# A fused attention and two-layer expert kernel: a least length for TensorE's runs of network products, and the plan's lengths of attention steps set anew

## The chip, the cores and the metric

One core of one Trainium2 chip runs the whole kernel. The metric is device time in microseconds (us), the median of the runs of one program. The engines are TensorE (PE in the profile; PEld is its weight load), VectorE (DVE), ScalarE (ACT), GpSimd (POOL) and SyncE (SP), which issues most DMA transfers.

## The reference

Attention on q, k and v of shape (4, 8, 576, 64), the sum of a pooled part and a banded part, feeds two networks one after the other; everything is float32.

```python
# pooled: mean over 4 neighbours, full attention on 144 positions, repeated 4 times
out_up = np.repeat(sm_attn(q_d, k_d, v_d), 4, axis=2)
# banded: softmax over the positions with |i - j| < 4
mask = np.abs(pos[:, None] - pos[None, :]) < 4
scores = np.where(mask, scale * np.matmul(q, k.transpose(0, 1, 3, 2)), -1e9)
x = (out_up + softmax(scores) @ v)            # as 2304 tokens x 512
g = x @ w_gate                                 # 512 -> 1536
x = (g * sigmoid(g) * (x @ w_val)) @ w_out     # 1536 -> 512
h = np.maximum(x @ w_in, 0.0)                  # 512 -> 2048
return h * h @ w_out2                          # 2048 -> 512
```

## The kernel before

The 2304 tokens are cut into nine tiles of 256 (`T1`). A float32 product is made of three float32r matmuls of 128x256 (`three`, lines 1045 to 1047), on operands split into a high and a low half. A product step of the first network (`gate`, `val` or `out_` in `unit_tasks`) is twelve of them: four blocks of 128 rows, three matmuls each. It is the unit in which network products are ordered. The first two tiles have four units (three product steps each) at first, later tiles six.

Attention makes the tiles. For each of the four batches there are four pooled tasks (`global_tasks`: one score step for two pairs of heads, then for each of its two halves a transpose step and a value step, lines 797, 816 and 835) and six banded tasks (`local_task`: a score step at line 649, a transpose step at line 686, a value step at line 707; the masked form of the first two batches also has one or two bfloat16 matmuls at line 644). Between these steps DVE and ACT do the softmax. The score and value steps work on 64 or 72 rows, the banded transposes on all 128, the pooled transposes on 72. `to_x` (line 725) adds both parts into the tile `xt`, of which there are two; when a tile is whole, ACT and DVE split it into `xs` (lines 1015 and 1019) and its product steps can begin.

The order of all instructions is worked out by a planner when the program is built (class `Order`). It keeps a clock for each engine, a list of times at which buffers come free, and for each task a list of `Stage`s with an engine, a planned length, and the buffers that it takes and gives. `next` takes the engine whose earliest stage starts first, lets all stages that could start within `LOOK` of it compete (0.05 us on TensorE), and decides by `rank`. On TensorE attention goes ahead of products as long as the attention steps since the last product (`streak`) are planned at less than `ATT_MAX`, 2.0 us; then products go first. `run` emits the chosen stage, so what it picks is the order in which each engine's queue is filled, SP's and POOL's DMA queues among them. Before a planned clock of 40 us `fill`, and up to 100 us `fill_bank`, put matmuls on zeros (lines 1251 and 81) where TensorE would wait. Nothing at run time reorders: a wrong planned length shows as a wait, or as a result that lies ready.

Four PSUM banks serve attention (`N_ATT`), two hold `gate` and `val` (`N_GV`), five buffers `p` and two `pt` pass the softmax on. Behind attention (270 us on) the rest of the span is network products alone.

Of the kernel before, what the change touches and what calls it, by code (L numbers as in the profile page):

```python
# [22 lines left out]
POOL = 4  # L23
# [27 lines left out]
QB = 1  # L51
# [12 lines left out]
def attn_moe_kernel(ctx: ExitStack, tc: tile.TileContext, qT, kT, vw, vin, vp, qp, kp, qs, ks, vs, maskc, masks, identc, wB, wC, out):  # L64
# [34 lines left out]
        return size / RATE  # L99

    AFTER = {"v": 0.15, "a": 0.2, "p": 0.2, "t": 0.25}
    ATT_MAX, LOOK_V, LOOK_A, LOOK_P, LOOK_T, LOOK_D, PE_MARGIN = 2.0, 0.1, 0.0, 0.2, 0.05, 0.6, 0.1
    PAD_END, PAD_WAIT, PAD_SHARE = 100.0, 0.6, 0.8
    TICK, FILL_END, BUSY = 10.24 / 3, 40.0, 3180
    W_DUE0, W_STEP, X_DUE0, X_STEP, X_STEP0 = 17.0, 2.2, 12.0, 20.0, 14.0
    S_DUE, S_STEP = 140.0, 15.0
    CUT_T, CUT_J, W_LAG, Q_LATE, Q_LATER, MASK_PE = 2, 4, 65.0, 10.0, 6.0, 2
    V_LATE, V_LATE1, V_LATE0, V_LEAD, W_LEAD, LEAD, LATE = -15.0, -10.0, -5.0, 1000.0, 1000.0, 80.0, 500.0
# [18 lines left out]
    def after(ts):  # L127

        return max([0.0] + [t.ready for t in ts]) if all(t.done for t in ts) else None

    class Order:
        def __init__(self):
            self.flying = []
            self.queues = {k: [] for k in ("x", "qk", "sum", "rows", "v", "att", "w", "mlp", "other", "done", "put")}
            n = {"att": N_ATT, "y": N_Y, "gv": N_GV, "p": N_P, "pt": N_PT, "v": N_V, "xt": N_XT}
            n |= {"sg": N_SG}
            self.free = {k: [0.0] * c for k, c in n.items()}
            self.named = {k: [(0.0, i) for i in range(n_[0])] for k, n_ in NAMED.items()}
            self.got = {k: [] for k in NAMED}
            self.clock = {e: 0.6 for e in "vaptd"}  # L140
            self.pad = 0
            self.load, self.filler, self.streak, self.landed = {}, None, 0.0, 0.0

        def hot(self, t):
# [59 lines left out]
        def next(self):  # L204

            found = {}
            heads = [(q[0], q) for q in self.queues.values() if q]
            for task, q in [(t, None) for t in self.flying] + heads:
                t = self.start(task)
                if t is None:  # L210
                    continue
                e = task.stages[task.at].engine
                if e is None:
                    return task, q, t, None
                wait = PE_MARGIN if e == "t" and not task.products else 0.0
                found.setdefault(e, []).append((max(t + wait, self.clock[e]), task, q, t))
            assert found, "no stage can go on"
            first = min(found, key=lambda e: min(c[0] for c in found[e]))
            limit = min(c[0] for c in found[first]) + LOOK[first]

            def rank(c):
                task = c[1]
                if task.products:
                    return (1 if first == "t" and self.streak < ATT_MAX else -1), task.due
                return 0, task.due

            _, task, q, t = min((c for c in found[first] if c[0] <= limit), key=rank)
            return task, q, t, first

        def run(self):  # L230
            while self.flying or any(self.queues.values()):
                task, q, t, engine = self.next()
                if q is not None:
                    q.pop(0)
                    self.flying.append(task)
                if task.at == 0:
                    self.flying += task.then
                s = task.stages[task.at]
                if engine == "t" and (task.products or self.clock["t"] >= FILL_END) and self.clock["t"] < PAD_END:
                    self.fill_bank(t, s)  # L240
                for k in s.take:
                    if k in self.named:
                        slot = min(self.named[k])
                        self.named[k].remove(slot)
                        self.got[k].append(slot[1])
                    else:
                        self.free[k].remove(min(self.free[k]))
                if engine == "t" and self.clock["t"] < FILL_END:
                    self.fill(max(t, self.clock["t"]), task)
                s.fn()  # L250
                if engine is not None:
                    c, cost = max(t, self.clock[engine]), s.cost
                    if engine == "t":
                        cost = self.columns(c, cost, s.share)
                        self.streak = 0.0 if task.products else self.streak + cost
                    self.clock[engine] = c + cost
                    t = c + cost + AFTER.get(engine, 0.0) + s.late
                    if engine == "d":

                        t = self.landed = max(c + FLIGHT, self.landed) + cost  # L260
                        self.clock["d"] = max(c + ISSUE, self.landed - AHEAD)
                        t += SLACK if c > FIRST else 0.3
                    if engine == "p":

                        self.landed = max(c + FLIGHT, self.landed) + dma(128 * HP * SD) * ACC
                        self.clock["d"] = max(self.clock["d"], self.landed - AHEAD)
                        t = max(t, self.landed + SLACK)
                task.ready = t
                task.times.append(t)
                task.at += 1  # L270
                for k in s.give:
                    if callable(k):
                        name, slot = k()
                        self.named[name].append((t, slot))
                    else:
                        self.free[k].append(t)
                if task.done:
                    self.flying.remove(task)
# [67 lines left out]
    att = tc.alloc_tile_pool(name="att", bufs=1)  # L346
# [267 lines left out]
    def local_task(b, i, ins, due, bls=(0, 1), early=False):  # L614

        u = {}
        first, last = early and i == 0, early and i == 2
# [8 lines left out]
        nb, b0 = len(bls), bls[0]  # L626
        n = nb * HP
# [118 lines left out]
        v_take = () if last else ("v",)  # L746
        v_in = Task([Stage("d", dma(128 * 512) * (1 if b < NB else 2), values, v_take, cond=lambda: task.ready)], due)
        if mask_pe:
            cost, share = 0.737 * nb, 0.74
            softmax = softmax_stages(u, n, 128, WIN, "s", float(D) ** -0.5, 1, False, ("att",))  # L750
        else:
            cost, share = 0.63 * nb, 0.68
            softmax = [Stage("v", dve(n * WIN), masked, (), ("att",))]
            softmax += softmax_stages(u, n, 128, WIN, "p", 1.0, 1, False, ())
        p_take, pt_take, pt_give = ("p",), ("pt",), ("pt",)
        if early:
# [6 lines left out]
                Stage("t", 0.22 * nb, trans, ("att",) + pt_take, p_take[-1:] * (not early), turn, 0.98),  # L763
                Stage("a", act(n * WIN, True), turned, (), ("att",)),
                Stage(
                    "t", 0.64 * nb, pv, ("att",), pt_give + v_take, ready, 0.62
                ),
                Stage("v", dve(232 * nb), to_x, (), ("att",)),
            ],
# [7 lines left out]
    def global_tasks(b, ins, due, combos, end=False):  # L777

        us = {}
        n = len(combos)  # L780
        cost = n * 0.26 * (POOL if b < QB else 1)

        def scores():
            for h2 in range(2):
                us[h2]["ps"] = bank("att")
                us[h2]["s"] = us[h2]["ps"][:QC, : n * SD].rearrange("p (c k) -> p c k", k=SD)
            for ci, (hp, qc) in enumerate(combos):
                for i in range(POOL if b < QB else 1):
                    for h2 in range(2):
                        r = slice(64 * h2, 64 * h2 + 64)  # L790
                        if b < QB:
                            c = qc * S // 2 - HALF0[qc] + i
                            q = q_t[b, qc][r, hp, c : c + S // 2 - POOL + 1 : POOL]
                        else:
                            q = qd_t[b][r, hp, qc * QC : qc * QC + QC]
                        start, stop = i == 0, b >= QB or i == POOL - 1
                        nc.tensor.matmul(us[h2]["s"][:, ci], q, kd_t[b][r, hp, :], start=start, stop=stop)  # L797

        first = Task(
            [Stage("t", cost, scores, ("att", "att", "p", "p"), (lambda: ("ys", 0),) * end, lambda: after(ins + [consts]), 0.92)],  # L800
            due,
        )
        for h2 in range(2):
            us[h2] = {}
            first.then = (*first.then, global_task(b, h2, us[h2], [first], due, combos))
        return first

    def global_task(b, h2, u, ins, due, combos):
        n = len(combos)
# [33 lines left out]
        def to_g():  # L843
            for r in range(2):
# [12 lines left out]
        task = Task(  # L857
            softmax_stages(u, n, QC, SD, "s", scale, POOL, True, ("att",), lambda: after(ins))
            + [
                Stage("t", 0.12 * n, trans, ("att", "pt"), ("p",), share=0.54),  # L860
                Stage("a", act(w, True), turned, (), ("att",)),
                Stage("t", (0.15 if apart else 0.2) * n, pv, ("att",), ("pt",), lambda: after(v_need), 0.84),
                Stage("a", halves * 0.051 + n * QC / 1200, to_g, (), ("att",)),
            ],
            due,
# [1577 lines left out]
```

## Time and profile before

| | |
|---|---|
| median of 3 runs | 943.97 us (943.89 to 944.54) |
| the profiled execution | 943.21 us, of which the span of the profile is 941.4 us |
| PE busy | 931.3 us, 99% |
| DVE busy | 758.2 us, 81% |
| ACT busy | 583.4 us, 62% |
| mean granted TensorE clock | 0.999 |

A busy PE says little here, since matmuls are pipelined and a matmul of 128x256 is shown with 0.28 us while one starts every 0.118 us. What matters is the distance from one matmul's start to the next one's, read from the order in time.

### The profile page before, as it was taken

What the parts mean: (1) busy time and instruction counts of PE and PEld (TensorE: products, weight loads), DVE (VectorE), ACT (ScalarE), POOL (GpSimd) and SP (SyncE); (2) the same over time, 40 slices, a digit from 0 to 9 for tenths busy, and PEclk for the clock granted to TensorE, in tenths of its full rate; (3) what the DMA queues carried; (4) which work ended last, traced back from release to release, by engine and by line L of the source; (5) the groups of instructions that cost most, each with busy time, mean ns of one, the idle gap of its engine ahead of it and who ended that gap; (6) DMA issues with size and microseconds to landing.
All of it is one profiled execution on the core that took longest, in us unless ns stands there. A gap on an engine that the chain in (4) does not pass through costs nothing.

```text
span 941.4 us, 22569 instructions
## 1 busy us (share of the span) xinstructions
PE 931.3 (99%) x8929; PEld 906.5 (96%) x8929; DVE 758.2 (81%) x1875; ACT 583.4 (62%) x1368; POOL 23.8 (3%) x31
## 2 busy tenths in 40 slices
PE   8999999999999999999999999999999999999997
PEld 7888999999999999999999999999999999999997
DVE  7998979778977788888896999968777667786775
ACT  4878566757666888466543575757565645445553
POOL 0102102000000000000000000000000000000000
PEclk9999999999999999999999999999999999999999
DMA  9998969485788756167462638614414864516131
GB/s 303 258 292 217 255 166 261 158 295 155 254 284 279 245 177 238 65 224 223 169 210 75 235 132 316 236 74 171 146 57 179 315 228 175 180 67 247 46 134 68
DMA packets 101205, 183.82 MB, mean 195 GB/s; under 512 B 22380, under 2 KB 60012, under 8 KB 101100
## 3 DMA queue, kind: packets, MB, share of 16 engines
q1 hardware_dynamic: 97644, 174.42, 54.7%
q0 software_dynamic: 3456, 7.96, 4.8%
q8 instruction: 70, 1.15, 0.5%
q14 instruction: 35, 0.29, 0.1%
HBM read 120.75 MB, written 61.60 MB: 194 GB/s over the span
## 4 chain that ended last, share of the span: by engine, by line
PE 96%; DVE 2%; ACT 1%; issue 0%; DVEq 0%
PE gv L1045 11%; PE gv L1046 11%; PE gv L1047 11%; PE y L1045 8%; PE y L1046 8%; PE y L1047 8%; PE att L1982 6%; PE att L1981 6%; PE att L1980 6%; PE att L1046 3%; PE att L1047 3%; PE att L1045 3%; PE att L707 2%; PE att L649 2%; PE att L797 2%; PE y L1251 2%
## 5 line engine op out<-in xcount | busy, mean ns | idle before, releaser
L1045 PE MATMUL gv<-xs,wg 128*128 128x256 f32 x880 | 250.5, 285 | 0.1
L1046 PE MATMUL gv<-xs,wg 128*128 128x256 f32 x880 | 247.0, 281 | 0.0
L1047 PE MATMUL gv<-xs,wg 128*128 128x256 f32 x880 | 246.8, 280 | 0.0
L1045 PEld LDWEIGHTS gv<-xs,wg 128*128 128x128 f32 x880 | 166.2, 189 | 2.3 <-DVE sg L1089 0.4
L1047 PEld LDWEIGHTS gv<-xs,wg 128*128 128x128 f32 x880 | 166.0, 189 | 0.0
L1046 PEld LDWEIGHTS gv<-xs,wg 128*128 128x128 f32 x880 | 166.0, 189 | 0.0
L2131 ACT ACTIVATE f<-rr 128x512 fp32r<-128x512 f32 (+2 forms) x200 | 87.8, 467 | 68.2 <-PE att L1982 32.2
L1982 PE MATMUL att<-wg,f 128*128 128x256 f32 x432 | 122.5, 284 | 0.5 <-DVE f L2134 0.4
L1980 PE MATMUL att<-wg,f 128*128 128x256 f32 x432 | 121.7, 282 | 0.3 <-ACT f L2131 0.3
L1981 PE MATMUL att<-wg,f 128*128 128x256 f32 x432 | 122.0, 282 | 0.0
L2134 DVE TENSOR_TENSOR f<-rr,f 128x512 fp32r<-128x512 f32 (+2 forms) x200 | 94.6, 490 | 29.5 <-ACT f L2131 28.4
L2055 ACT ACTIVATE rr<-rr 128x512 f32<-128x512 f32 (+1 forms) x144 | 79.8, 556 | 36.8 <-DVE rr L2058 35.0
L1046 PE MATMUL y<-xs,wg 128*128 128x256 f32 x336 | 94.7, 282 | 1.1 <-DVE xs L1570 1.1
L1045 PE MATMUL y<-xs,wg 128*128 128x256 f32 x336 | 94.6, 281 | 0.0
L1047 PE MATMUL y<-xs,wg 128*128 128x256 f32 x336 | 94.3, 281 | 0.0
L1982 PEld LDWEIGHTS att<-wg,f 128*128 128x128 f32 x432 | 81.2, 188 | 1.4 <-DVE f L2134 1.3
L1980 PEld LDWEIGHTS att<-wg,f 128*128 128x128 f32 x432 | 81.8, 189 | 0.6 <-ACT f L2131 0.6
L1981 PEld LDWEIGHTS att<-wg,f 128*128 128x128 f32 x432 | 81.5, 189 | 0.0
L2140 DVE TENSOR_TENSOR rr<-rr 128x256 f32<-128x256 f32 (+1 forms) x160 | 62.6, 393 | 9.1 <-ACT rr L2055 7.1
L1046 PEld LDWEIGHTS y<-xs,wg 128*128 128x128 f32 x336 | 63.5, 189 | 1.5 <-DVE xs L1570 1.5
L1045 PEld LDWEIGHTS y<-xs,wg 128*128 128x128 f32 x336 | 63.6, 189 | 0.4 <-ACT ys L1228 0.2
L1047 PEld LDWEIGHTS y<-xs,wg 128*128 128x128 f32 x336 | 63.5, 189 | 0.0
(149 smaller groups left out, 2316.8 us busy)
## 6 DMA issues: line engine op xcount, KB each, us to landing
wst<-wB SPq DMA_DIRECT2D x36, 512.0 KB, 5.0
w_sp<-tmp SPq DMA_DIRECT2D x36, 512.0 KB, 3.6
wg<-w_sp SPq DMA_DIRECT2D x36, 512.0 KB, 4.9
wst<-wC SPq DMA_DIRECT2D x32, 512.0 KB, 5.2
y_sp<-ys SPq DMA_DIRECT2D x29, 512.0 KB, 4.5
xf_sp<-xs SPq DMA_DIRECT2D x24, 512.0 KB, 2.7
xs<-xf_sp SPq DMA_DIRECT2D x24, 512.0 KB, 5.8
ys<-y_sp SPq DMA_DIRECT2D x20, 512.0 KB, 6.8
```

The lines of the kernel that those rows point to most:

```text
L649: nc.tensor.matmul(u["s"][r, c * HP + hp], q[r, hp, q0 - o : q0 - o + WIN], k[r, hp, w0 - o : w0 - o + WIN], start=not mask_pe, stop=not m ...
L707: nc.tensor.matmul(ps[rr, o : o + t1 - t0], u["v"][rr, bls[c], hpp, h2, :], pt[rr, c, hpp, h2, t0 - q0 : t1 - q0], start=True, stop=True,)
L1045: nc.tensor.matmul(o, w[:, 0], x[:, 0], start=start, stop=False, skip_group_check=more)
L1046: nc.tensor.matmul(o, w[:, 0], x[:, 1], start=False, stop=False, skip_group_check=more)
L1047: nc.tensor.matmul(o, w[:, 1], x[:, 0], start=False, stop=stop, skip_group_check=more)
L1980: nc.tensor.matmul(o, h, w[:, 0], start=first and not again and c == 0, stop=False, skip_group_check=again)
L1981: nc.tensor.matmul(o, h, w[:, 1], start=False, stop=False, skip_group_check=again)
L1982: nc.tensor.matmul(o, l, w[:, 0], start=False, stop=end, skip_group_check=again)
L2055: return lambda: nc.scalar.activation(out=whole(f, c0), in_=whole(f, c0), func=func)
L2131: nc.scalar.activation(out=fac(k, 0), in_=source(), func=AF.Copy)
L2134: nc.vector.tensor_tensor(out=fac(k, 1), in0=source(), in1=fac(k, 0).bitcast(F32), op=ALU.subtract)
L2140: go = lambda: nc.vector.tensor_tensor(out=o(), in0=a(), in1=b(), op=op)
```

## The change

The diff changes the planner and nothing of what is computed. `ATT_MAX` goes from 2.0 to 4.0 us. The planned clock gets 0.1 us (`SWITCH`) whenever TensorE goes from products to attention or back. A new count, `stay`, holds the planned length of products since the last attention step; from a planned clock of 70 us on, and while no attention step has run since the last product, products go ahead of attention until it has reached 4.0 us. The planned lengths of the attention steps are new: for two blocks of a banded task the masked scores go from 1.474 to 1.30 us, the others from 1.26 to 1.08, values from 1.28 to 1.07; for one block they go from 0.737 to 0.83, 0.63 to 0.61 and 0.64 to 0.60; the pooled scores go from 2.08 to 2.34 us in the first batch and from 0.52 to 0.64 in the others, a pooled transpose step from 0.24 to 0.25 and a pooled value step from 0.3 to 0.4.

```diff
-    ATT_MAX, LOOK_V, LOOK_A, LOOK_P, LOOK_T, LOOK_D, PE_MARGIN = 2.0, 0.1, 0.0, 0.2, 0.05, 0.6, 0.1
+    ATT_MAX, LOOK_V, LOOK_A, LOOK_P, LOOK_T, LOOK_D, PE_MARGIN = 4.0, 0.1, 0.0, 0.2, 0.05, 0.6, 0.1
+    SWITCH, STAY, STAY_FROM = 0.1, 4.0, 70.0
-            self.pad = 0
+            self.pad, self.stay, self.mode = 0, 0.0, False
                 if task.products:
-                    return (1 if first == "t" and self.streak < ATT_MAX else -1), task.due
+                    stay = self.stay < STAY and self.clock["t"] > STAY_FROM and self.streak == 0.0
+                    return (1 if first == "t" and self.streak < ATT_MAX and not stay else -1), task.due
                     if engine == "t":
+                        c += SWITCH * (self.mode != task.products)
+                        self.mode = task.products
                         cost = self.columns(c, cost, s.share)
+                        self.stay = self.stay + cost if task.products else 0.0
                         self.streak = 0.0 if task.products else self.streak + cost
-            cost, share = 0.737 * nb, 0.74
+            cost, share = 0.36 + 0.47 * nb, 0.74
-            cost, share = 0.63 * nb, 0.68
+            cost, share = 0.14 + 0.47 * nb, 0.8
-                    "t", 0.64 * nb, pv, ("att",), pt_give + v_take, ready, 0.62
+                    "t", 0.13 + 0.47 * nb, pv, ("att",), pt_give + v_take, ready, 0.74
-        cost = n * 0.26 * (POOL if b < QB else 1)
+        cost = n * (1.17 if b < QB else 0.32)
-                Stage("t", 0.12 * n, trans, ("att", "pt"), ("p",), share=0.54),
+                Stage("t", 0.125 * n, trans, ("att", "pt"), ("p",), share=0.54),
-                Stage("t", (0.15 if apart else 0.2) * n, pv, ("att",), ("pt",), lambda: after(v_need), 0.84),
+                Stage("t", (0.2 if apart else 0.25) * n, pv, ("att",), ("pt",), lambda: after(v_need), 0.84),
```

## Rows read from the trace of the kernel before

**Rows 1.** The page: span, and busy time of each engine.
```profile
span 941.4 us, 22569 instructions
...
PE 931.3 (99%) x8929; PEld 906.5 (96%) x8929; DVE 758.2 (81%) x1875; ACT 583.4 (62%) x1368; POOL 23.8 (3%) x31
```
**Rows 2.** Stretches: length, busy PE, PEld, DVE, ACT, POOL, clock, DMA share, GB/s.
```profile
33.90:68.77 34.87, 34.85 (x455) 31.09 (x455) 32.80 (x88) 26.08 (x75) 4.29 (x5) 1.00 0.97 292
68.77:107.67 38.90, 38.67 (x532) 34.86 (x529) 36.38 (x95) 30.79 (x86) 7.82 (x9) 1.00 0.94 240
107.67:158.97 51.30, 51.28 (x682) 48.05 (x680) 41.91 (x118) 34.35 (x100) 6.94 (x8) 1.00 0.82 209
```
**Rows 3.** PE in time order (start, us, line, tiles, shape, count): one product run between visits.
```profile
152.51 0.28 PE L1047 MATMUL y<-hh,wg 128*128 128x256 f32 x1
152.63 0.60 PE L686 MATMUL att<-ident,p 128*128 128x128 f32 x4
152.98 0.36 PE L1045 MATMUL gv<-xs,wg 128*128 128x256 f32 x1
153.18 0.28 PE L1046 MATMUL gv<-xs,wg 128*128 128x256 f32 x1
...
154.36 0.28 PE L1047 MATMUL gv<-xs,wg 128*128 128x256 f32 x1
154.56 1.14 PE L707 MATMUL att<-pt,vw 64*64 64x58 f32 x32
155.64 0.66 PE L686 MATMUL att<-ident,p 128*128 128x128 f32 x4
156.22 1.15 PE L649 MATMUL att<-kT,qT 64*64 64x64 f32 x32
157.30 0.39 PE L1045 MATMUL y<-hh,wg 128*128 128x256 f32 x1
```
**Rows 4.** PE in time order: one value step alone, then like steps side by side.
```profile
131.23 0.47 PE L835 MATMUL att<-pt,vd 72*64 72x72 f32 x8
131.63 0.44 PE L816 MATMUL att<-ident,p 72*72 72x72 f32 x4
...
140.26 0.72 PE L835 MATMUL att<-pt,vd 72*64 72x72 f32 x16
140.91 2.08 PE L649 MATMUL att<-kT,qT 64*64 64x64 f32 x64
142.92 0.39 PE L1045 MATMUL y<-hh,wg 128*128 128x256 f32 x1
```
**Rows 5.** PE in time order: first and last of 48 attention visits from 70 us.
```profile
71.80 0.72 PE L835 MATMUL att<-pt,vd 72*64 72x72 f32 x16
...
268.69 1.14 PE L707 MATMUL att<-pt,vw 64*64 64x58 f32 x32
```
**Rows 6.** Time order, all engines: the last steps before the third tile's products.
```profile
99.61 1.15 PE L649 MATMUL att<-kT,qT 64*64 64x64 f32 x32
...
106.83 0.68 DVE L1019 TENSOR_TENSOR xs<-xt,xs 128x512 fp32r<-128x512 f32 x1
```
**Rows 7.** PE in time order: where a long product run halts.
```profile
161.78 0.28 PE L1047 MATMUL gv<-xs,wg 128*128 128x256 f32 x1
162.13 0.39 PE L1045 MATMUL gv<-xs,wg 128*128 128x256 f32 x1
162.35 0.28 PE L1046 MATMUL gv<-xs,wg 128*128 128x256 f32 x1
```
**Rows 8.** Groups of PE instructions (count, busy us, mean ns, idle before): zeros that fill waits.
```profile
L81 PE MATMUL gv<-zeros 128*128 128x256 bf16 x21 | 2.6, 273 | 0.0
```
**Rows 9.** Waits (who, for whom: us, times, longest): first 70 to 300 us, then all.
```profile
PE att L835 <- ACT pt L822: 0.2, 1, 0.2
...
PE y L1046 <- DVE xs L1570: 1.1, 2, 0.6
PE y L1045 <- ACT ys L1228: 0.8, 1, 0.8
```

## The prediction

> **What bounds the kernel now.** First the page: TensorE is busy 931.3 of 941.4 us, the next engine, DVE, 758.2 [rows 1]. So the end is set by what TensorE's queue holds and how closely it runs, and a shorter attention step elsewhere is worth nothing by itself. Second the waits: from 70 to 300 us TensorE waited 0.2 us for anybody; over the whole span the longest sums are 1.1 and 0.8 us, both after attention [rows 9]. So almost nothing is to be had from waits where the change acts. Third the stretches: while attention runs, the clock is 1.00 and TensorE full, but DVE is at 32.80 of 34.87 and 36.38 of 38.90 us in the first two of them and 41.91 of 51.30 in the third [rows 2]. It is a second engine near its limit early on. Fourth the order in time, which shows what a full TensorE hides. Inside a run of products one matmul starts every 0.118 us (153.18 to 154.36 is ten). The first one of a run holds the second up until 0.20 us after it, and the last one is followed by a 64-row step 0.20 us after its start, but by a 128-row transpose 0.12 us after it (152.51 to 152.63) [rows 3]. So each visit of attention costs 0.08 us on the way back to products, and 0.08 us on the way in if it begins with a 64-row step. The run of twelve in the rows takes 1.58 us from start to start, 0.16 more than 12 x 0.118. That is what the change can win.
>
> **The visits removed.** From 70 us there are 48 visits [rows 5] and between them 47 product runs with 1,092 matmuls: 35 runs of 12 matmuls, four of 24, eight of 36 to 144 (576 matmuls in all). The new rule lets attention in only after 4.0 us of products. A product step is planned at 12 x 0.118 = 1.41 us, two are 2.83, so it takes three: runs of 36. If the eight long runs stay as they are, the other 516 matmuls make 14 runs, and 22 runs are left; if all runs shrink to the least length, 1,092 / 36 = 30. So 17 to 25 visits go. I take 21, the middle: the long runs come where no attention step can start, and they will shrink by part of what the short ones gain.
>
> **What one is worth.** The 35 runs of 12 average 1.575 us, 0.16 us over the steady pace, and the row read above is one of them [rows 3]. Against this stands what the joined visits pay among themselves. A transpose of 128 rows takes 0.35 us ahead of products (152.63 to 152.98) and 0.58 ahead of a 64-row step (155.64 to 156.22) [rows 3]: 0.23 more, so the way in is then paid inside the visit. Like steps side by side save: a banded score step alone takes 1.08 us (156.22 to 157.30), two together 2.01 [rows 3, 4]; a pooled value step 0.40, two 0.65 [rows 4]: 0.15 us each time. About two visits in three begin with a 64-row step and half end in a transpose, whose extra over both kinds of transposes averages 0.17; a like step follows in some 15 of 100. So a merge keeps 0.16 - 0.68 x (0.5 x 0.17 - 0.15 x 0.15) = 0.12 us. Bounds for one merge: 0.03 if each new neighbour costs what the way in cost, 0.16 if none does. The sum: 21 x 0.12 = 2.5 us gained; 17 x 0.03 = 0.5 and 25 x 0.16 = 4.0 at the ends.
>
> A rule of the Trainium skill bears on this. TensorEngine Tiling (Array Packing), Key Properties, says that changing the tiling mode, and not merely the tile, drains TensorE. The entry into the 128-row transposes, 0.12 us, agrees; the 0.20 us on the way back from them (152.98 to 153.18) doesn't follow from it, since both sides use the whole array [rows 3]. By this rule alone a merge would save no drain where visits mix 128-row and 64-row steps, and the time would be that of the second rival below.
>
> **Before 70 us.** Here only `ATT_MAX`, `SWITCH` and the new lengths act. With 4.0 instead of 2.0 us two score steps of the first batch can follow each other, and perhaps two visits are joined, 0.2 us. But this stretch is held by others: DVE at 94% and the DMA engines at 0.97 [rows 2], and TensorE had room for 2.6 us of zero matmuls that fill planned waits [rows 8]. I take a gain of 0.2 and bounds of 1.5 us either way, a bit over half of those zeros, since a new order can shed or add them.
>
> **Planned lengths.** The new numbers are those of the rows: 1.08 us for banded scores, planned at 1.26 before; 0.40 for a pooled value step, planned at 0.3; 0.2 us for a return trip, planned at none [rows 3, 4]. The plan's TensorE thus keeps step with the real one. That removes no wait, as there was only 0.2 us [rows 9]; it can add some, because before, returns left out of the plan (48 x some 0.16 = 8 us by the end) made TensorE arrive later than planned, with the results of DVE and ACT already there. Work queued behind such a wait is everything on TensorE, in order. Bound: none, or the halt that a long product run shows now, 0.35 + 0.22 - 2 x 0.118 = 0.33 us [rows 7], which two of the eight long runs have; at that rate 18 more runs of 36 would lose 1.5 us. The halts come 24 matmuls or more into a run, where a run of 36 is nearly over, so I take 0.2.
>
> **What is moved.** Attention steps that wait for three product steps delay what hangs on them. Score steps free `kT` and `qT` and the pooled sums, so the next loads on SP's and POOL's queues go out up to 4.2 us later; the DMA engines are at 0.94 and then 0.82 in those stretches [rows 2], so they come later but needn't crowd. `xt` and its spill move with the last value step of a tile. None of these had TensorE waiting, so I cost them at nothing except in the third tile. Its split ends at 106.83 + 0.68 us [rows 6], and from 68.77 to 107.67 us the products come from tile two alone: twelve steps and three left of tile one, of which 14 were used. The stock was all but gone as the next tile came. If products are taken in threes, 14 steps last five visits, and the 38.90 - 14 x 1.41 - 2.2 (13 returns) = 17 us of attention in this stretch must go at 3.4 us a visit. The new `ATT_MAX` allows that, four PSUM banks and two `pt` buffers may not. What is left would run without products between. I take a loss of 0.2, with a bound of 4 product steps, 5.6 us (third rival). After that tiles three and four put 36 product steps in stock, and it isn't short again.
>
> **Sum.** -2.5 - 0.2 + 0.2 + 0.2 = -2.3 us. Against the profiled execution that is 941.4 - 2.3 = 939.1 us of span and 943.21 - 2.3 = 940.9 us; the median stood 0.76 us above that execution, so 943.97 - 2.3 = 941.7 us. Within 0.2% (1.9 us, about what a measurement of this kernel can tell from no change) means 942.1 to 945.9.
>
> **Rivals.**
> 1. Forecast: visits merge, nothing runs dry. 941.7 us, alone 939.5 to 943.4. For it: every product run of twelve shows the same 0.10 to 0.2 us, and TensorE has no waits in the way. Chance 0.60, of which 0.45 lies below 942.1.
> 2. The drains move inside the visits, or the rule seldom bites because the product that it prefers isn't ready within 0.05 us. Then 0.5 us or less is won: 943.4 us. For it: 0.58 against 0.35 us behind a transpose [rows 3], and DVE's load, which can hold `gv`. Against it: product runs of up to 144 matmuls go with two halts. Chance 0.14.
> 3. Slower: the third tile. The products of tile two are eaten in threes, and the last banded step's chain, from its scores at 99.61 to the split's end at 107.5 us [rows 6], runs with an idle TensorE where it now has four product steps. It decides once visits from 70 to 107 us stay below 3.4 us of attention. Price 4 x 1.41 = 5.6 us; less the 2.5 won elsewhere: 943.97 + 3.1 = 947.1 us. For it: DVE at 36.38 of 38.90 us [rows 2], which such a chain needs. Against it: TensorE's total is the same, and a product step that isn't there makes the rule void. Chance 0.26.
>
> **How the numbers follow.** Faster by over 0.2%: 0.45, from the first. Same: 0.15 of the first, 0.12 of the second, 0.03 of the third, 0.30. Slower: 0.02 and 0.23, 0.25. The range leaves out the lowest of the first case and the upper half of the third: 939.3 to 947.1.
>
> **What would show it.** In the changed profile, from 70 us to the end of attention: 22 to 30 product runs, hardly one below 36 matmuls; attention visits of 2.5 us and more with like steps side by side; the same 0.118 us inside runs. If the runs are there and the time isn't, the rows to look at are waits of TensorE before 110 us, zeros of line 81, and halts inside runs. The forecast is wrong if runs of 12 stay the rule, if TensorE's waits from 70 to 300 us exceed 1.5 us, or if the third tile's split ends after 109 us.

## The result, and the profile after

The changed kernel takes 952.02 us (median of 4 runs, 950.17 to 953.37) against 943.93 us (943.55 to 944.54) beside it on the same chip: 1.0084 times as long, 95% interval 1.0064 to 1.0104. It is slower by 8.1 us. The forecast was 2.3 us faster, its range ended at 947.1 us.

The page of the profiled execution (950.17 us; the one of before took 943.21), span and busy time by engine:

```profile
span 948.4 us, 22570 instructions
...
PE 933.8 (98%) x8926; PEld 907.9 (96%) x8926; DVE 759.0 (80%) x1875; ACT 583.4 (62%) x1368; POOL 23.7 (2%) x31
```

Beside [rows 1] the span grew by 7.0 us and TensorE's busy time by only 2.5. So most of the loss is time in which TensorE stands, and the waits of TensorE from 70 to 300 us, where before had 0.2 us [rows 9], say where (for whom and by whom, us, times, longest):

```profile
PE gv L1050 <- DVE sg L1094: 3.6, 1, 3.6
```

One wait of 3.6 us. TensorE in order of time around it (start, us, line, shape, count, idle before), and two stretches (length, busy PE, PEld, DVE, ACT, POOL, clock, DMA share, GB/s):

```profile
275.43 0.28 PE L1052 MATMUL gv<-xs,wg 128*128 128x256 f32 x1
279.28 0.38 PE L1050 MATMUL gv<-xs,wg 128*128 128x256 f32 x1 [3.57 <-DVE sg L1094]
...
282.40 0.41 PE L1050 MATMUL gv<-xs,wg 128*128 128x256 f32 x1
282.62 0.41 PE L1051 MATMUL gv<-xs,wg 128*128 128x256 f32 x1
...
283.39 0.28 PE L1050 MATMUL gv<-xs,wg 128*128 128x256 f32 x1
283.50 0.28 PE L1051 MATMUL gv<-xs,wg 128*128 128x256 f32 x1
```
```profile
275.00:280.00 5.00, 1.43 (x11) 1.22 (x10) 4.37 (x9) 5.00 (x10) 0.00 (x0) 0.96 0.84 257
280.00:285.00 5.00, 5.00 (x33) 5.00 (x32) 2.95 (x8) 3.55 (x8) 0.00 (x0) 0.70 0.79 308
```

Behind the wait some 17 matmuls go every 0.21 us instead of 0.118, at a granted clock of 0.5 (1.2 GHz), until 283 us: the wait costs 3.6 us and the clock 1.6 behind it.

**Where the 7.0 us are.** The start of each product matmul in the two traces was compared, the same one in both (there are 6,792). The changed kernel is behind by 2.97 us at the end of attention, by 8.24 us some 46 matmuls on, by 8.09 at 357 us, and by 6.9 to 7.0 from 363 us to the end. So 3.0 us are lost while attention runs, 5.3 us in the wait and the clock behind it, and 1.1 us come back where before itself waits 0.8 us, at 358 us, for `ys` [rows 9]. The median shows another 1.1 us over this that the two profiled executions don't hold, and no trace shows where they are lost; the two longest of the four runs (952.82 and 953.37 us) have a mean granted clock of 0.996, the other two 0.998.

**While attention runs** each stretch from one start to the next on TensorE is put to the instruction that opens it, up to the end of attention (269.8 us before, 271.2 after, where 12 matmuls fewer were done). The table is divided where both kernels have done the same attention steps, at the visit that begins at 71.80 us before [rows 5] and at 76.28 us after:
```profile
76.28 0.72 PE L840 MATMUL att<-pt,vd 72*64 72x72 f32 x16
```

| us | before, to 71.8 | after, to 76.3 | before, from there | after, from there |
|---|---|---|---|---|
| attention steps | 32.2 | 33.6 | 60.7 | 64.2 |
| zeros (all lines) | 19.8 | 20.0 | 0 | 0 |
| products over 0.1174 us each | 2.0 | 3.4 | 9.0 | 5.3 |
| visits | 21 | 24 | 48 | 29 |

At the dividing line the changed kernel has done 12 product matmuls more and is behind by 76.28 - 71.80 - 12 x 0.1174 = 3.1 us; at the end of attention it is behind by 2.9 us, counted in the same way. So what is lost while attention runs is lost ahead of the visits that the rule joins, and these visits win 0.2 us in all. (Two executions of the same order differ by some 0.5 us in these figures.)

**Up to 76 us** TensorE has waits in the changed kernel that the one before has not; both have the 2.4 us for ACT's zeros at the start (waits from 0 to 70 us, after and then before):
```profile
PE y L1256 <- ACT zeros L1250: 2.4, 1, 2.4
PE att L840 <- ACT pt L827: 1.0, 2, 0.6
PE att L654 <- DMA qT<-qT: 0.4, 1, 0.4
PE y L1052 <- DVE wg L431: 0.2, 1, 0.2
```
```profile
PE y L1251 <- ACT zeros L1245: 2.4, 1, 2.4
```
Without that one they sum to 1.6 us. The lag jumps from 1.0 us (at 58 us) to 2.8 us at 73 us, where 25 zeros stand in front of the second tile's first products. There are fewer zeros in all than before, 150 for 153, but they stand later.

**From 76 us on** the product runs won more than was forecast of them, 3.7 us. Attention lost 3.5 us. How, one joined visit of the changed kernel shows (PE in order of time):

```profile
151.26 0.47 PE L840 MATMUL att<-pt,vd 72*64 72x72 f32 x8
151.66 0.44 PE L821 MATMUL att<-ident,p 72*72 72x72 f32 x4
152.03 1.15 PE L654 MATMUL att<-kT,qT 64*64 64x64 f32 x32
153.11 0.47 PE L840 MATMUL att<-pt,vd 72*64 72x72 f32 x8
153.51 0.44 PE L821 MATMUL att<-ident,p 72*72 72x72 f32 x4
153.88 1.15 PE L654 MATMUL att<-kT,qT 64*64 64x64 f32 x32
154.96 0.44 PE L821 MATMUL att<-ident,p 72*72 72x72 f32 x4
155.34 0.47 PE L840 MATMUL att<-pt,vd 72*64 72x72 f32 x8
155.74 0.38 PE L1050 MATMUL y<-hh,wg 128*128 128x256 f32 x1
155.96 0.28 PE L1051 MATMUL y<-hh,wg 128*128 128x256 f32 x1
...
160.16 0.47 PE L840 MATMUL att<-pt,vd 72*64 72x72 f32 x8
```

Between 155.74 and 160.16 stands a run of 36 matmuls in 4.42 us, as the rule wants. But the visit ahead of it changes its kind of step seven times, never two alike side by side. Counted from the dividing line to the end of attention: changes from one kind of attention step to another went from 50 to 76, and their cost from 8.57 to 12.25 us (from the start of a step's last instruction to that of the next kind). Ahead of the line they are 22 in both kernels, at 4.1 and 4.0 us. The ends of visits fell from 48 to 29, and their cost by only 0.8 us, from 4.47 to 3.69. For most of the ends that went were cheap: transposes that go to products fell from 24 to 8, at 0.03 us each, while transposes followed by another attention step rose from 13 to 27, at 0.15 and 0.16. The rule named in the prediction (the Trainium skill, TensorEngine Tiling (Array Packing), Key Properties: a change of tiling mode drains TensorE) agrees with these rows: from 72-row transposes (72*72) to 64-row steps a change costs 0.16 us, from banded scores to banded values, which are both shown with 64*64, only 0.05 us.

**The wait at 275 us** is not one of attention's. ACT in order of time, then SP's DMA issues:

```profile
274.93 0.63 ACT L1359 ACTIVATE tmp<-wf 128x512 fp32r<-128x512 f32 x1 [3.81 <-DMA w_sp<-tmp]
275.47 0.76 ACT L372 ACTIVATE bits<-wst 128x512 fp8e5<-128x512 f32 x1
276.10 2.16 ACT L1020 ACTIVATE xs<-xt 128x512 fp32r<-128x512 f32 x4
278.17 0.36 ACT L1086 ACTIVATE sg<-gv 128x256 f32<-128x256 f32 x1
```
```profile
264.18 0.74 SPq L450 DMA_DIRECT2D w_sp<-tmp  x1
267.56 0.33 SPq L1338 DMA_DIRECT2D wst<-wC  x1
268.16 3.43 SPq L450 DMA_DIRECT2D w_sp<-tmp  x2
```

When attention is done, its pool of memory is given up and a new one takes its place (`late()`). Buffer 5 of `tmp` lies in the old pool. Its last store is the second of the two issued from 268.16 us on, and the first write into the new memory, the ACTIVATE at 274.93, waits 3.81 us for it. Behind it in ACT's order stand a weight conversion, four splits of tiles (2.16 us) and only then the tanh of L1086, which frees the `gv` bank for which TensorE stands. In the kernel before, the stores of that time went out from 263.58 us on (SP; the trace leaves buffer numbers out, so which of them is that of buffer 5 isn't shown), and TensorE has no wait there [rows 9]:
```profile
263.58 2.05 SPq L445 DMA_DIRECT2D w_sp<-tmp  x2
```
The plan doesn't hold this wait: `late` lets the new buffers be free when attention's tasks end, while by the same plan the store is done later. That it is some 8 us later is a figure of the plan, which no trace shows; the expectation for the version with `ATT_MAX` 2.0 below gives it.

### The profile page after: what moved, and what is told of

It is laid out like the page before. It is cut to its first block, busy times and chain, and to the rows that moved or that the text cites. A ratio compares the mean times of both kernels' runs of the same rounds, so it can differ in the third digit from the quotient of the medians.

```text
span 948.4 us, 22570 instructions
## 1 busy us (share of the span) xinstructions
PE 933.8 (98%) x8926; PEld 907.9 (96%) x8926; DVE 759.0 (80%) x1875; ACT 583.4 (62%) x1368; POOL 23.7 (2%) x31
## 4 chain that ended last, share of the span: by engine, by line
PE 89%; DVE 5%; ACT 4%; DMA 1%; issue 1%; SPq 0%; ACTq 0%; DVEq 0%
PE gv L1050 10%; PE gv L1051 10%; PE gv L1052 10%; PE y L1050 8%; PE y L1051 8%; PE y L1052 8%; PE att L1987 6%; PE att L1986 6%; PE att L1985 6%; PE att L1051 3%; PE att L1052 3%; PE att L1050 3%; PE att L654 2%; PE att L712 2%; PE att L840 1%; PE att L691 1%
## 5 line engine op out<-in xcount | busy, mean ns | idle before, releaser
L2136 ACT ACTIVATE f<-rr 128x512 fp32r<-128x512 f32 (+2 forms) x200 | 87.8, 467 | 68.3 <-PE att L1987 32.2
```

The costliest lines, as they stand in the source:

```text
L2136: nc.scalar.activation(out=fac(k, 0), in_=source(), func=AF.Copy)
```

## The experiments

Four theories: **1**, the handover of attention's memory; **2**, the rule lets products run out while a tile is awaited; **3**, the new lengths and `SWITCH` take away TensorE's lead over its plan, so it waits more; **4**, changes of the kind of step cost what the visits saved. All versions compute the same. Ratios are against the kernel before, run beside them.

**The memory handed over earlier.** In the changed kernel:
```diff
-    late_ = Task([apart("tmp", 5, turned_all), apart("bits", 1), Stage(None, 0.0, late)])
+    early = lambda: after(att_tasks[B - 2])
+    late_ = Task([apart("tmp", 5, early), apart("bits", 1, turned_all), Stage(None, 0.0, late)])
```


> The changed kernel, but the one stream buffer that lies in attention's memory (tmp 5) is taken out of use when the third batch's attention is done, and not after the last one's; all steps up to the end of attention stay in the same order. Theory 1 (memory handed over): 5.4 us of the loss are one halt of TensorE at 275 us, where the first write into memory that attention gives up waits for the last store out of it, issued at 271.03 and landed at 274.93. That store is now some 45 DMA issues earlier, so the halt goes: 946 to 947.5 us, attention still ending near 271 us. Theory 2 (the new rule starves the products, which the halt only shows): the halt moves and stays, 950 to 953 us.


948.92 us, 1.0048 [1.0033, 1.0063]. The wait shrinks to 1.1 us; ACT no longer waits for the store, and what is left is its four splits ahead of the tanh (waits from 70 to 300 us; ACT in order of time):
```profile
PE gv L1050 <- DVE sg L1094: 1.1, 1, 1.1
```
```profile
272.73 0.78 ACT L372 ACTIVATE bits<-wst 128x512 fp8e5<-128x512 f32 x1
273.37 2.17 ACT L1020 ACTIVATE xs<-xt 128x512 fp32r<-128x512 f32 x4
275.44 0.36 ACT L1086 ACTIVATE sg<-gv 128x256 f32<-128x256 f32 x1
```
At 285 us it is 4.5 us ahead of the changed kernel, of which 0.5 us are there during attention already, where both have the same order; waits of 0.5, 0.8 and 0.4 us at 358 to 362 us, which the changed kernel, being later there, doesn't have, take 2.2 of them back. Theory 1 holds, though the time lies above the 946 to 947.5 us that it expected, and 3.4 us of the 8.1 are its net share.

**The change without its rule.** `STAY` 4.0 → 0.0:


> The changed kernel without the new rule (STAY 0): ATT_MAX 4.0, SWITCH and new lengths stay. Visits from 70 us on: about 42. Theory 1: the last store out of attention's memory is again issued shortly ahead of the last two tiles' spills (three issues), so a halt of 2 to 4 us again at the end of attention: 947 to 952 us. Theory 2: without the rule no halt, 943 to 945 us.


956.40 us, 1.0126 [1.0111, 1.0141]: slower than with the rule. So the rule isn't what makes the change slow; beside the other edits it wins 4 us. Both expectations missed: the longest wait behind attention is 1.4 us and not 2 to 4, but this version is 3.2 us behind before at 76 us already, and 6.5 us at the end of attention.

**The rule alone.** The kernel before with `STAY` (old lengths, `ATT_MAX` 2.0, `SWITCH` 0):


> The kernel before with the new rule alone (STAY 4.0 from 70 us; ATT_MAX 2.0, SWITCH 0, old lengths). Theory 1: fewer visits win 1.5 to 2.5 us; the last store out of attention's memory stands between the spills of the last two tiles and the first write into that memory comes five ScalarE instructions behind the first split, so the halt is 0 to 3 us: 941.5 to 945 us. Theory 2: 948 us and more, since the rule alone starves the products.


948.92 us, 1.0048 [1.0033, 1.0063]. Here the third tile starves (waits from 100 to 115 us, then stretches as above):
```profile
PE gv L1050 <- ACT xs L1020: 1.5, 1, 1.5
PE gv L1051 <- DVE xs L1024: 0.8, 1, 0.8
```
```profile
105.00:110.00 5.00, 3.40 (x69) 2.57 (x67) 5.00 (x11) 2.90 (x6) 1.67 (x2) 0.93 1.12 252
110.00:115.00 5.00, 4.29 (x20) 4.29 (x21) 5.00 (x13) 1.53 (x3) 0.00 (x0) 0.50 1.05 295
```
The clock is at half from the wait on for 6.8 us. This is the prediction's third rival, in a version that has `ATT_MAX` as before. Up to 73 us it is 0.4 us behind before, with the same order, so the rule has no part in what the changed kernel loses there.

**`ATT_MAX` 4.0 alone**, on the kernel before:


> The kernel before with ATT_MAX 4.0 alone. Both theories see little before 70 us: some visits join, 943 to 944.5 us. Theory 1: the last store out of attention's memory is issued four issues ahead of the spills, five in the kernel before, so a halt of 0 to 2 us may come: up to 946 us.


946.65 us, 1.0029 [1.0017, 1.0040]. Attention's changes of kind rise from 72 to 85 and cost 14.70 us instead of 12.69, and attention ends 1.5 us later at an equal count of products, with waits of 0.56 us in all (0.43 before). But 1.4 of these 1.5 us are there at 73 us, where 5 of the 13 new changes have come, and the other 8 cost the 1.0 us that the products win. Theory 4 fits the size; that it is the cause was not tested here.

**The new lengths alone**, on the kernel before:


> The kernel before with the new planned lengths alone (no STAY, SWITCH 0, ATT_MAX 2.0). Theory 3 (lost lead): in the kernel before, TensorE ran 7.6 us behind its plan by the end of attention, so results lay ready; true lengths take that lead away, and TensorE waits or idles more: 2 to 4 us slower, 946 to 948.5 us. Theory 1 adds no halt here (last store out of attention's memory four issues ahead of the spills, as in the run with ATT_MAX alone). If neither holds: 943.5 to 945 us.


950.16 us, 1.0069 [1.0042, 1.0095]. The edit, as the change itself, holds two more numbers, the shares by which the plan books a banded step as activity of TensorE (0.68 to 0.80 and 0.62 to 0.74). The profiled execution is the longest of the four (954.75 us). In it TensorE waits 5.5 us before attention's end, besides the 2.4 us at the start, where before has 0.2 (1.1 us each at 10 and 15 us, 1.7 at 68 us), and 1.8 us at 283 us; it is 7.0 us behind before at 80 us and 6.6 at attention's end. So theory 3's sign is there, above the size that it expected. Numbers closer to the trace made a slower order.

**`SWITCH` 0.1 alone**, on the kernel before:


> The kernel before with SWITCH 0.1 alone. Theory 1: the last store out of attention's memory is issued right ahead of the last tiles' spills, and the first write into that memory stands ahead of the splits in ScalarE's queue, as in the changed kernel: a halt of 3 to 5 us behind the end of attention, 948 to 951 us. Theory 3: half of the lead gone, 1 to 2 us. If neither: 944 to 945 us.


954.67 us, 1.0108 [1.0093, 1.0123]. Its plan had the store of `tmp` 5 late, and the wait came, longer than in the changed kernel (ACT in order of time; waits of TensorE; one stretch):
```profile
278.36 0.63 ACT L1359 ACTIVATE tmp<-wf 128x512 fp32r<-128x512 f32 x1 [6.41 <-DMA w_sp<-tmp]
```
```profile
PE gv L1050 <- DVE sg L1099: 4.5, 1, 4.5
```
```profile
280.00:285.00 5.00, 4.30 (x20) 4.30 (x21) 4.04 (x10) 2.71 (x8) 0.00 (x0) 0.50 0.64 216
```
It is 4.8 us behind before at attention's end (2.0 of them by 70 us) and 11.9 some 46 matmuls on: 7.0 us in one place. Theory 1 again: the wait was foretold from the plan, in its size too, though the time lies above the expected 948 to 951 us.

**Like steps first.** The first version, and the kernel before, with an order among attention steps that could start now:
```diff
-                return 0, task.due
+                kind = task.stages[task.at].fn.__qualname__ if first == "t" else ""
+                return 0, (0 if kind == self.last else 2 if kind.endswith("trans") else 1) if first == "t" else 0, task.due
```
(Cut: the lines that note `self.last`, the kind of TensorE's last step, and a 0 put in the same place for products. Due times only break ties.)


> The run e1 (the changed kernel with the buffer taken out early), and in a visit the plan takes, among the attention steps that can start, first one of the kind just done, and transposes last. Visits stay about as many (33 for 29). Theory 4 (what costs is the change from one kind of step to another, on either side of a visit's border): fewer changes inside visits, summed from the rows of before and after 21.1 us for 25.1, so 4 us less up to the end of attention: 944 to 946 us. The forecast's view (visits cost, neighbours hardly): as e1, 948 to 949.5 us.


949.14 us, 1.0046 [1.0030, 1.0063]: no gain on the median over the version without it. Yet changes of kind fell from 97 to 75, and what attention's end lies behind that of before, at an equal count of products, from 2.3 to 1.0 us. In the profiled execution, the longest of the four (951.13 us), a wait of 2.2 us at 391 us, for ACT's `h`, and 3.4 us of half clock behind it then took 5.0 us; nothing of that is attention's.


> The kernel before, with the same preference for like steps and transposes last. Theory 4: 23.3 us of changes for 24.2, so 0.9 us less up to the end of attention; theory 1: the last store out of attention's memory three issues ahead of the spills and the first write ahead of the splits, so a halt of 0 to 3 us: 943 to 946 us.


944.00 us, 1.0000 [0.9986, 1.0013]. Changes of kind fell from 72 to 62 and attention ended 1.1 us earlier at an equal count of products; by the end the profiled execution was 0.5 us behind, with waits of 0.6 us at 277 and 0.5 at 355 us among what gave it back. Theory 4 holds for attention itself, at 1.3 of the 4 us that were expected in the first version and 1.1 for 0.9 in the second; the median shows nothing of it.

**The rules with the old lengths.** The first version with the old planned lengths and `SWITCH` 0:


> The changed kernel with `tmp` 5 taken out early (as in the run before with that edit, 948.9 us), and beside it the old planned lengths and no SWITCH: only STAY and ATT_MAX 4 are left of the change. Theory 3 (the new lengths and SWITCH take away the lead that the real TensorE had over its plan, so it waits more): waits of TensorE before the end of attention fall from 1.84 us to below 1 us, the same 30 visits from 70 us on; 948.9 - 1.3 = 947.6 us. With it theory 4 (each change of kind of step costs 0.08 to 0.17 us; the plan has 0.6 us less of them): 947.0 us. Theory 1 (memory handed over behind attention): the halt near 276 us, 1.1 us in that run, stays below 1.5 us. Rival (lengths and SWITCH only change the order, and the loss is the rule's own): the waits stay near 1.8 us, and the time is 948.9 us or more.


947.95 us, 1.0033 [1.0019, 1.0047]; the interval overlaps with that of the first version. The waits before attention's end did not fall (2.1 us, 1.84 there). The time lies near the 947.6 us that theory 3 expected, but by luck, as the waits that were to bring it didn't change. So theory 3 falls beside the rules: there the lengths and `SWITCH` cost at most about 1 us, and not by waits before attention's end. Attention takes 97.4 us and the products' excess is 8.73 us, about as in the changed kernel (97.8 and 8.73): neither needs the new lengths or `SWITCH`.

**The change with `ATT_MAX` 2.0:**


> The whole change but for ATT_MAX, which stays at 2.0. Theory 2 (the rule lets the products run out while the third tile is awaited, and a longer limit for attention averts it): TensorE waits 2 us or more near 109 us for the third tile's splits, with a clock at half behind it, which the changed kernel doesn't have: 3 to 6 us. Theory 1: the plan has the handover of attention's memory ready 1 us after its end instead of 8 us, so the halt of 3.6 us and the clock behind it (5.3 us together) go. The two nearly cancel: 950 to 953 us, with a lag of 3 to 6 us more at 115 us than the changed kernel has. Rival (ATT_MAX does nothing for the third tile): no wait of 1 us from 100 to 115 us, and 947 us.


949.07 us, 1.0046 [1.0031, 1.0061], below what was expected. The third tile starves (waits from 100 to 115 us; a stretch), and in the waits from 270 to 300 us there is no row left:
```profile
PE gv L1050 <- ACT xs L1020: 1.1, 1, 1.1
PE gv L1051 <- DVE xs L1024: 0.5, 1, 0.5
```
```profile
110.00:115.00 5.00, 3.67 (x17) 3.47 (x18) 5.00 (x13) 2.19 (x5) 0.88 (x2) 0.66 1.09 266
```
So `ATT_MAX` 4.0 is what keeps the third tile fed under the rule (no wait there in the changed kernel), and the wait of the handover goes without its edit when the plan has the store done early.

**A version after the theories:** the kernel before with `STAY` 2.8 from 110 us on, like steps first, `tmp` 5 out early:


> A version after the theories: the kernel before with the rule at 2.8 us of products instead of 4.0 and from 110 us on instead of 70, so that the third tile keeps its stock; old lengths, ATT_MAX 2, no SWITCH; among attention steps that could start the one like the last comes first and transposes last (into products); `tmp` 5 taken out when the third batch's attention is done. Theory 4 (changes of step cost): the plan has 22.6 us of such costs where the kernel before has 24.2, so TensorE leads the kernel before by 1.6 to 2.5 us at the end of attention. Theory 1: no halt over 1.5 us near 270 to 280 us. Together 942 to 943 us. Rival (whatever is won before attention's end is given back behind it, as in the like-step version of the kernel before): 944 us and within 0.1% of the kernel before.


944.11 us, 0.9990 [0.9980, 1.0000]. Its page:
```profile
span 942.4 us, 22550 instructions
...
PE 929.3 (99%) x8917; PEld 906.5 (96%) x8917; DVE 757.9 (80%) x1875; ACT 583.6 (62%) x1368; POOL 23.8 (3%) x31
```
At attention's end it leads before by 2.4 us at an equal count of products; a wait of 1.3 us at 277 us for the tanh behind the four splits, and 1.7 us of waits at 354 to 358 us where before has 0.8, give most of it back. By the median 0.1% is left, which this measurement hardly tells from nothing; against the changed kernel it is 8 to 9 us. The rival half of the expectation came true: attention was won, the time was not.

## Why the prediction was wrong

- **What bounds the kernel** stood: TensorE's order, and closely run. But from the 0.2 us of waits it was read that none would come. They were the state of one planned order, not a property of the stage: each edit of the plan drew another one, and with the lengths, `SWITCH` or the rule alone there are single waits of 1.5 to 4.5 us before 300 us.
- **The visits removed:** 17 to 25, taken 21; measured 19, and 24 of 36 matmuls. Right.
- **What one is worth:** 0.12 us kept, at least 0.03. Measured: 0.2 us for 19 visits, 0.01 each. This is the first failed step. The products' side was a little better than its 0.16 us (3.7 us, 0.19 a merge). Against it the sum set 0.04 us a merge for what moves inside visits; attention lost 3.5 us, 0.18 a merge, and its changes of kind cost 3.7 us more. Two errors in it: only transposes were charged for a neighbour, though nearly every step pays about 0.15 us when another kind follows; and it was taken that half of the ends that go are transposes, while they were 16 of 19, at 0.03 us the cheapest.
- **The second rival** named this mechanism, with a gain of 0.5 us or less and a chance of 0.14. For the joined visits that is what the runs show, in mechanism and price.
- **Before 70 us:** -0.2, bounds of 1.5. Measured: 3.1 us lost by the time of the first visit behind that stretch, twice the bound. This is the second failed step. Waits of 0.4, 0.6 and 0.4 us stand at 8, 28 and 44 us, and the second tile's splits come 3.8 us later, so that 25 zeros hold its place where before had 6 (PE, ACT in order of time, after and then before):
```profile
70.30 2.89 PE L81 MATMUL gv<-zeros 128*128 128x256 bf16 x25
...
71.45 1.15 ACT L1020 ACTIVATE xs<-xt 128x512 fp32r<-128x512 f32 x2
```
```profile
67.65 1.13 ACT L1015 ACTIVATE xs<-xt 128x512 fp32r<-128x512 f32 x2
...
68.19 0.82 PE L81 MATMUL gv<-zeros 128*128 128x256 bf16 x6
```
  It looked at the third tile for what happened to the second, and its bound was taken from the 2.6 us of one group of zeros [rows 8], while all zeros of that stretch take 19.8 us. Each edit of the plan that acts here loses something by 70 to 80 us when alone: `ATT_MAX` 1.4 us, `SWITCH` 2.0, the lengths 7.0 in a long execution; the rule, which does not act here, 0.4. By what way the new order makes the second tile late was not tested and stays open.
- **Planned lengths:** 0.2 for halts, bounds of nothing and 1.5. Alone they cost 0.69%, beside the rules at most about 1 us. The reason given (a lost lead makes waits) fits the version with the lengths alone, with 5.5 us of waits before attention's end, beyond the bound; beside the rules it was tested and not borne out.
- **What is moved** was costed at nothing outside the third tile, with the loads on SP's queue named. This is the third failed step, and the largest: the stores on that queue were not followed to the one whose memory is handed over. It cost 5.3 us.
- **The third tile:** 0.2 us, and no more: its splits end at 106.67 + 0.7 us. The rival's condition, visits below 3.4 us, was right: the long visits that `ATT_MAX` 4.0 allows averted it, and with 2.0 it came, twice.
- **What would show it:** runs of 36 are there, but only 8 of the 29 visits last 2.5 us or more, like steps stand seldom side by side in them, and the bound on TensorE's waits, 1.5 us, is passed by one wait of 3.6.

In sum, up to the first joined visit -0.2 was forecast and +3.1 found; for the joined visits, with halts and the third tile, -2.1 was forecast and -0.2 found; behind attention nothing was forecast and +5.3 - 1.1 found. The median adds 1.1 that stays open, as does what sets the waits at 354 to 369 us, by which most versions fall 0.7 to 2.4 us further behind between 300 and 370 us.

## What to carry to other kernels

When runs of one kind of work are made longer on an engine, price what the other kind does inside its own longer runs, by the pairs of steps that will meet, and see which borders go: the cheap ones may. In an order drawn up by a planner each number redraws everything behind it, so the cover of every wait of before is to be looked up again, above all where one stage's memory passes to the next and a single store holds up an in-order engine. When a loss is to be explained, find first the moment from which it is there, by comparing both kernels where they have done the same work: the 26 new changes of kind here cost more than all that was lost while attention ran, and yet that loss stood before they came. And a lead won in one stage counts only if the next stage can take it.

## What the runs showed of the hardware

From the start of an attention step's last instruction to that of the first one of another kind TensorE takes 0.15 to 0.16 us behind banded scores, banded values, pooled values and 72-row transposes, 0.20 from a 128-row transpose into scores or values, 0.21 behind pooled scores and 0.24 behind mask rows (averages over both kernels, where nothing is waited for). It takes 0.05 us from banded scores to banded values and 0.03 us from a transpose into products. Inside a step the distance is 0.03 us for the banded steps and the pooled values, 0.07 for pooled scores and 72-row transposes and 0.12 for 128-row transposes.

Behind waits of 3.6 us (changed kernel) and 2.2 us (like steps first) the granted clock stood at 0.5, which is 1.2 GHz, for 3.4 us. It stood there for 6.8 us with the wait of 4.5 us in the version with `SWITCH` alone, and with 1.5 and 0.8 us close together in the one with the rule alone. Single waits of 1.1 to 1.6 us at 276 to 288 us went by without it; one of 1.1 with 0.5 behind it at 111 us did not, and neither did one of 1.8 us at 283 us in the version with the lengths alone. The clock added 1.6 us to the wait in the changed kernel and 2.5 in the version with `SWITCH` alone (7.0 lost, 4.5 of them waiting).
